# Joining the kv products of two batches, calling the second batch's load three slots sooner, and spacing batch 2's x pieces one and a half units apart

## The chip, the cores and the metric

The kernel runs on one core of one Trainium2 chip. The time is the device time of that core in microseconds (us). Each kernel is run several times; medians and ranges are given. The traced span is 1.7 to 1.9 us shorter than the device time of the same run, so spans are compared only with spans.

## The reference

Linear attention with an RMS norm over each head, then a bilinear feed-forward layer:

```python
# q, k, v: (batch 8, heads 8, seq 576, dim 64); 8*576 = 4608 tokens of 512 features
kv  = np.einsum('bhsd,bhse->bhde', k, v)
out = np.einsum('bhsd,bhde->bhse', q, kv)
x   = out / np.sqrt(np.mean(out*out, axis=-1, keepdims=True) + 1e-06) * g_norm
x   = x.transpose(0, 2, 1, 3).reshape(4608, 512)
y   = (x @ w_a) * (x @ w_b) @ w_out       # w_a, w_b: 512 x 1536, w_out: 1536 x 512
```

## The kernel before

The feed-forward layer goes over the 4608 tokens in 9 strips of 512. A strip is 12 "units" (four products with `wa` and four with `wb`, 1.73 us together) and 4 output groups of 12 products. While strip s runs, attention for batch s+1 is woven into the stream of TensorE in "slots" n, one per unit or group, with half slots in the middle. For batches 2 to 7 the woven pieces are:

- `kv`: one run of 40 small products (128x64 weights, two heads side by side in the two column halves) into PSUM bank 7, then copies to SBUF;
- five x pieces `c` of 128 tokens (the last has 64): `tx` (product and square), `tss` (row sums), `trs` (reciprocal root, and a scaling product on POOL), `txt` (multiply on VectorE, which frees the PSUM bank, and a transposing DMA into `xt`). Piece c uses bank 5 + c % 3, so piece 3 needs the bank of piece 0.

```python
    def load_late(b):                       # on POOL: q, k, v of batch b
        if b > EARLY:
            nc.gpsimd.tensor_copy(gate, qT[(b - 1) % 2][0:1, 0, 0:1])   # waits: q of b-1 transposed
        d = qs_d[b].rearrange("t (h d) -> t h d", h=H)
        for hs in (slice(0, NP), slice(NP, H)):
            nc.gpsimd.dma_start(out=d[:, hs, :], in_=q[b, hs].rearrange("h t d -> t h d"))
        n = 128 * LC
        for t, src in ((ktl[b % 2], k), (vtl[b % 2], v)):
            nc.gpsimd.dma_start(out=t[:, :, 0:LC, :], in_=...)          # 512 rows
            nc.gpsimd.dma_start(out=t[0 : S - n, :, LC, :], in_=...)    # the other 64
    ...
    def slot(A, s, n):
        kb = P[:, 7, 0 : NP * D].rearrange("q (p e) -> q p e", e=D)
        k0, xs = (5, (6.5, 7.5, 8.5, 9.5, 10.5)) if s == 1 else (2, (3.5, 5, 6, 7.5, 8.5))
        if n == k0:
            for p in range(NP):
                A.kv(p, kb[:, p, :])
            A.kv_out(slice(0, NP), kb)
        for c, x in enumerate(xs):
            i = 5 + c % 3
            if n == x:         A.tx(c, i)
            elif n == x + 0.5: A.tss(c)
            elif n == x + 1:   A.trs(c)
            elif n == x + 2.5: A.txt(c, i)
    ...
            if s == 1 and n == 3:
                load_late(3)
            if b + 1 < B and n == (12 if s == 1 else 8):     # b = s + 1
                transpose_q(b + 1)
            if b + 2 < B and n == 13:
                load_late(b + 2)
```

Of the kernel before, what the change touches and what calls it, by code (L numbers as in the profile page):

```python
# [15 lines left out]
def kernel(  # L16
# [11 lines left out]
    nc = tc.nc  # L28

    B, H, S, D = q.shape  # L30
# [5 lines left out]
    NP = H // 2  # L36
# [12 lines left out]
    def sb(shape, dt, name):  # L49
        return pool.tile(shape, dt, name=name, tag=name)  # L50
# [19 lines left out]
    kvb = [sb([128, NP, 128], BF16, f"kvb{i}") for i in range(2)]  # L70
# [34 lines left out]
    P = psum.tile([128, 8, STRIP], FP32, name="P", tag="P")  # L105
# [27 lines left out]
    def load_late(b):  # L133
        if b > EARLY:

            nc.gpsimd.tensor_copy(gate, qT[(b - 1) % 2][0:1, 0, 0:1])
# [5 lines that stand above are left out]
            nc.gpsimd.dma_start(  # L142
                out=t[:, :, 0:LC, :],
                in_=src[b, :, 0:n].rearrange("h (t c) d -> t h c d", c=LC),
            )
            nc.gpsimd.dma_start(
                out=t[0 : S - n, :, LC, :], in_=src[b, :, n:].rearrange("h t d -> t h d")
            )

    def transpose_q(b):  # L150
        nc.sync.dma_start_transpose(qT[b % 2], qs_d[b])


    class Attn:
# [18 lines left out]
                        stop=(c == len(rows) - 1),  # L173
                    )

        def kv_out(self, ps, src):
            for j in range(2):
                r = slice(j * D, (j + 1) * D)
                nc.scalar.copy(kvb[self.b % 2][r, ps, r], src[r])  # L179


        def kv1(self, p, i):
# [118 lines left out]
    class Unit:  # L301
        n = 0
# [36 lines left out]
    def ab_bank():  # L339
        n_ab[0] += 1  # L340
        return AB[(n_ab[0] - 1) % len(AB)]

    def ffn_ab(s, fc, between=None):
        u = Unit(s, fc, ab_bank(), ab_bank())
        u.part_a()
        if between:
            between()
        u.part_b()
# [38 lines left out]
    def ffn_o(s, g, i=O, between=None):  # L387
        o_mm(s, g, i, range(FC // 2))
        if between:
            between()  # L390
        o_mm(s, g, i, range(FC // 2, FC))
        o_out(s, g, i)
# [46 lines left out]
    A = Attn(0)  # L439
# [22 lines left out]
    for j in range(2):  # L462
        r = slice(j * D, (j + 1) * D)
# [7 lines left out]
    for p in range(1, NP):  # L471
        i = X[p % 2]
# [42 lines left out]
    A = Attn(1)  # L515
# [30 lines left out]

    def slot(A, s, n):

        kb = P[:, 7, 0 : NP * D].rearrange("q (p e) -> q p e", e=D)
        k0, xs = (5, (6.5, 7.5, 8.5, 9.5, 10.5)) if s == 1 else (2, (3.5, 5, 6, 7.5, 8.5))  # L550
        if n == k0:
            for p in range(NP):
                A.kv(p, kb[:, p, :])
            A.kv_out(slice(0, NP), kb)
        for c, x in enumerate(xs):
            i = 5 + c % 3
            if n == x:
                A.tx(c, i)
            elif n == x + 0.5:
                A.tss(c)  # L560
            elif n == x + 1:
                A.trs(c)
            elif n == x + 2.5:
                A.txt(c, i)

    for s in range(1, N_STRIP - 1):
        b = s + 1
        A = Attn(b) if b < B else None
        for n in range(FC + 4):
            amid = (lambda n=n: slot(A, s, n - 0.5)) if A else None  # L570
            if n >= FC:
                ffn_o(s, n - FC, ab_bank() if n % 2 else O, amid)
            elif s > 1 or n > 1:
                ffn_ab(s, n, amid)
            if A:
                slot(A, s, n)

            if s == 1 and n == 3:
                load_late(3)
            if b + 1 < B and n == (12 if s == 1 else 8):  # L580
                transpose_q(b + 1)
            if b + 2 < B and n == 13:
                load_late(b + 2)
    last = N_STRIP - 1
    for fc in range(FC):
# [41 lines left out]
```

## Time and profile before

| reading | value | where |
|---|---|---|
| median time | 319.09 us (318.94 to 319.32, 6 runs) | runs |
| TensorE (PE) busy | 310.9 of 317.4 us | page, part 1 |
| a strip with one batch of attention (strip 3, 118.53 to 151.81) | 33.28 us | PE timeline |
| a strip without (strip 7, 251.65 to 282.73) | 31.08 us | PE timeline |
| one kv run of 40 products | 0.85 us | PE timeline |
| PE waits inside strips | two, 1.2 us, both in strip 1 | waits |

Part 1 of the page of the kernel before: busy us, share of the span, and instructions of each engine.

```profile
PE 310.9 (98%) x1907; PEld 147.6 (46%) x1907; DVE 138.2 (44%) x230; ACT 115.8 (37%) x229; POOL 101.8 (32%) x124
```

TensorE bounds it: nothing else is above 46%. So the question is where PE waits. The waits of PE in the kernel before: total us, times, longest us.

```profile
PE P L397 <- DVE eps_t L412: 1.2, 1, 1.2
PE P L258 <- DVE qv L292: 1.2, 2, 0.6
PE P L219 <- ACT sq L215: 0.4, 1, 0.4
```

Only the middle line lies in the strips: the x products (L258) wait for VectorE's `txt` (L292). The timeline of strip 1 of the kernel before shows how; columns are start, us, engine, line, operation, count, and in brackets the idle time before with what ended it.

```profile
68.10 0.72 POOL L146 DMA_DIRECT2D vtl<-in_v_dram  x1
...
68.80 2.08 POOL L282 TENSOR_TENSOR sqt<-rst,g_all 128x512 f32<-128x512 f32 x2
...
69.67 0.69 DVE L330 TENSOR_TENSOR ab<-P,asb 128x512 bf16<-128x512 f32 x1 [0.67 <-PE P L312]
...
70.28 0.68 DVE L292 TENSOR_TENSOR qv<-P,sqt 128x512 bf16<-128x512 f32 x1
...
71.01 0.38 PE L258 MATMUL P<-kvb,qT 128*128 128x128 bf16 x4 [0.58 <-DVE qv L292]
...
72.36 0.69 DVE L330 TENSOR_TENSOR ab<-P,asb 128x512 bf16<-128x512 f32 x1 [0.81 <-ACT sqt L265]
72.97 0.68 DVE L292 TENSOR_TENSOR qv<-P,sqt 128x512 bf16<-128x512 f32 x1
...
73.70 0.38 PE L258 MATMUL P<-kvb,qT 128*64 128x128 bf16 x4 [0.58 <-DVE qv L292]
```

The multiply of piece 0 ends at 70.96, and piece 3, due in the same bank at about 70.27, starts at 71.01. Piece 4 waits for piece 1's multiply in the same way.

POOL issues load 3 until 68.8 and so comes late to the scaling. The two scalings end at 69.9 and 70.9.

One kv run in the stream of PE, strip 3 of the kernel before:

```profile
122.85 1.03 PE L312 MATMUL P<-xt,wb_t 128*128 128x512 bf16 x4
123.81 0.82 PE L168 MATMUL P<-vtl,ktl 128*64 128x64 bf16 x40
124.56 1.04 PE L312 MATMUL P<-xt,wa_t 128*128 128x512 bf16 x4
```

Read starts, not durations (durations are of pipelined instructions). Four 512-wide products take 0.86 us, so without the kv run the next unit would start at 123.71. It starts at 124.56: the run costs 0.85 us, of which 0.10 us passes before its first product.

Now the load of batch 5, on POOL, in the kernel before:

```profile
106.76 1.04 POOL L282 TENSOR_TENSOR sqt<-rst,g_all 64x512 f32<-64x512 f32 x1 [1.19 <-ACT rst L275]
108.85 0.18 POOL L136 COPY gate<-qT 1x1 bf16<-1x1 bf16 x1 [1.05 <-DMA qT<-qs]
109.09 3.31 POOL L139 DMA_DIRECT2D qs<-in_q_dram  x2
112.39 0.91 POOL L142 DMA_DIRECT2D ktl<-in_k_dram  x1
113.29 0.70 POOL L146 DMA_DIRECT2D ktl<-in_k_dram  x1
113.96 0.91 POOL L142 DMA_DIRECT2D vtl<-in_v_dram  x1
```

And the view of the v tile in the same stretch:

```profile
DMA to landing us min/median/max: 12.5/12.7/12.9
```

So v of batch 5 lands at about 126.9 to 127.3 (113.96 + 12.9; its small rest is issued at 114.84). In the kernel before that is early: kv of batch 5 comes in strip 4, at 157.

### The profile page before, as it was taken

The numbers are of one execution on the slowest core, as the hardware profiler recorded it, in microseconds if no ns is written. First come the engines' busy times: TensorE is split into PE (matmuls) and PEld (weight loads), VectorE is DVE, ScalarE is ACT, GpSimd is POOL, SyncE is SP. The second block draws the span as 40 slices with busy tenths as digits, with TensorE's granted clock in tenths as the row PEclk, the third lists the DMA queues.
The fourth block names the chain that finished last, engine by engine and source line by source line (L and its number), as shares of the span: only waits on it lengthen the run. The fifth ranks groups of instructions, "written<-read, shape, count | busy, mean of one in ns | idle before, by whom it ended". The sixth has DMA issues, their size and how long they took to land.

```text
span 317.4 us, 4979 instructions
## 1 busy us (share of the span) xinstructions
PE 310.9 (98%) x1907; PEld 147.6 (46%) x1907; DVE 138.2 (44%) x230; ACT 115.8 (37%) x229; POOL 101.8 (32%) x124
## 2 busy tenths in 40 slices
PE   8999999999999999999999999999999999999995
PEld 3444454444445444544454445444544444444443
DVE  5543345367137613771258225741485144213421
ACT  3733155453246314640355025512461233123310
POOL 8944890193163550347023801310042000000000
PEclk9999999999999999999999999999999999999999
DMA  8999999999799799069916992363012300020002
GB/s 179 196 196 199 200 182 150 228 125 159 167 166 140 128 155 208 4 130 136 228 13 123 124 221 38 69 115 99 2 34 57 116 4 0 33 93 8 0 33 101
DMA packets 94237, 36.19 MB, mean 114 GB/s; under 512 B 64902, under 2 KB 89734, under 8 KB 94214
## 3 DMA queue, kind: packets, MB, share of 16 engines
q0 software_dynamic: 59120, 18.44, 53.4%
q1 hardware_dynamic: 34738, 17.01, 22.9%
q10 hardware_dynamic: 356, 0.43, 0.5%
q8 instruction: 15, 0.25, 0.3%
q14 instruction: 8, 0.07, 0.1%
HBM read 37.78 MB, written 12.98 MB: 160 GB/s over the span
## 4 chain that ended last, share of the span: by engine, by line
PE 85%; DMA 7%; POOL 4%; issue 1%; DVE 1%; ACT 0%; POOLq 0%; DVEq 0%
PE P L312 52%; PE P L369 28%; DMA wb_t<-in_moe_w_b_dram 6%; PE P L258 2%; PE P L168 2%; DMA vt<-in_v_dram 2%; POOL qt L116 1%; POOL wo_t L131 1%; POOL kt L116 1%; POOL vt L116 1%; POOL wa_t L427 0%; POOL wb_t L427 0%; DVE qv L292 0%; PE P L192 0%; PE P L219 0%
## 5 line engine op out<-in xcount | busy, mean ns | idle before, releaser
L330 DVE TENSOR_TENSOR ab<-P,asb 128x512 bf16<-128x512 f32 x108 | 74.5, 691 | 111.3 <-PE P L312 93.8
L312 PE MATMUL P<-xt,wa_t 128*128 128x512 bf16 x432 | 111.9, 379 | 0.0
L312 PE MATMUL P<-xt,wb_t 128*128 128x512 bf16 x432 | 111.7, 379 | 0.1
L326 ACT CAST asb<-P 128x512 bf16<-128x512 f32 x108 | 63.1, 586 | 91.2 <-PE P L312 91.2
L369 PE MATMUL P<-wo_t,ab 128*128 128x512 bf16 (+1 forms) x444 | 95.6, 373 | 0.0
L369 PEld LDWEIGHTS <-ab 128*128 128x128 bf16 x444 | 43.1, 98 | 49.1
L312 PEld LDWEIGHTS <-wa_t 128*128 128x128 bf16 x432 | 41.3, 98 | 47.1 <-issue 0.2
L312 PEld LDWEIGHTS <-wb_t 128*128 128x128 bf16 x432 | 41.2, 98 | 47.2 <-DMA wb_t<-in_moe_w_b_dram 0.6
L282 POOL TENSOR_TENSOR sqt<-rst,g_all 128x512 f32<-128x512 f32 (+1 forms) x24 | 25.0, 1044 | 97.4 <-ACT rst L275 97.4
L382 ACT COPY osb<-P 128x512 f32<-128x512 f32 x17 | 10.0, 586 | 74.2 <-PE P L369 59.6
L384 DVE COPY osb<-P 128x512 f32<-128x512 f32 x18 | 12.4, 691 | 47.2 <-PE P L369 42.6
L139 POOL DMA_DIRECT2D qs<-in_q_dram x12 | 19.8, 1655 | 1.2 <-issue 0.9
L271 DVE TENSOR_REDUCE sst<-sqt 128x8 f32<-128x512 f32 (+1 forms) x24 | 16.2, 676 | 0.8 <-ACT sqt L265 0.8
L292 DVE TENSOR_TENSOR qv<-P,sqt 128x512 bf16<-128x512 f32 (+1 forms) x24 | 16.2, 678 | 0.0
L265 ACT ACTIVATE sqt<-P 128x512 f32<-128x512 f32 (+1 forms) x24 | 14.2, 593 | 1.6 <-PE P L258 1.6
L258 PEld LDWEIGHTS <-qT 128*128 128x128 bf16 (+1 forms) x120 | 8.9, 100 | 9.5 <-issue 4.0
L258 PE MATMUL P<-kvb,qT 128*128 128x128 bf16 (+1 forms) x120 | 11.7, 220 | 1.2 <-DVE qv L292 1.2
L275 ACT ACTIVATE rst<-sst,eps_t 128x8 f32<-128x8 f32 (+1 forms) x30 | 9.0, 301 | 4.3 <-DVE sst L271 4.3
L179 ACT CAST kvb<-P 64x256 bf16<-64x256 f32 (+1 forms) x20 | 6.0, 301 | 11.3 <-PE P L168 11.2
L233 DVE SCALAR_TENSOR_TENSOR xt<-P,g_col,rs 128x288 bf16<-128x288 f32 x16 | 7.5, 512 | 5.2 <-ACT rs L223 5.2
L131 POOL DMA_DIRECT2D wo_t<-in_moe_w_out_dram x12 | 6.4, 533 | 6.7 <-DMA wb_t<-in_moe_w_b_dram 3.2
L282 POOL TENSOR_TENSOR k_x<-rst,g_all 128x512 f32<-128x512 f32 x6 | 6.3, 1044 | 7.0 <-ACT rst L275 7.0
(66 smaller groups left out, 120.4 us busy)
## 6 DMA issues: line engine op xcount, KB each, us to landing
out_dram<-osb SPq DMA_DIRECT2D x23, 256.0 KB, 2.4
qs<-in_q_dram POOLq DMA_DIRECT2D x12, 288.0 KB, 6.9
ktl<-in_k_dram POOLq DMA_DIRECT2D x6, 512.0 KB, 10.1
vtl<-in_v_dram POOLq DMA_DIRECT2D x6, 512.0 KB, 12.5
out_dram<-osb SPq DMA_DIRECT2D x13, 128.0 KB, 2.3
wo_t<-in_moe_w_out_dram POOLq DMA_DIRECT2D x12, 128.0 KB, 5.9
wa_t<-in_moe_w_a_dram POOLq DMA_DIRECT2D x5, 256.0 KB, 9.3
wb_t<-in_moe_w_b_dram POOLq DMA_DIRECT2D x5, 256.0 KB, 9.9
```

Source lines behind the costliest of these rows:

```text
L139: nc.gpsimd.dma_start(out=d[:, hs, :], in_=q[b, hs].rearrange("h t d -> t h d"))
L258: nc.tensor.matmul(P[0:n, i, p * 128 : (p + 1) * 128], lhsT=self.qT[:, p, t0 : t0 + n], rhs=kvb[self.b % 2][:, p, :], start=True, stop=True,)
L265: nc.scalar.activation(sqt[c % 3][0:n], P[0:n, i, :].rearrange("t (h d) -> t h d", h=H), AF.Square)
L271: nc.vector.reduce_sum(sst[c % 3][0:n], sqt[c % 3][0:n], axis=mybir.AxisListType.X)
L282: nc.gpsimd.tensor_mul(sqt[c % 3][0:n], rst[c % 3][0:n].unsqueeze(2).to_broadcast([n, H, D]), g_all[0:n].unsqueeze(1).to_broadcast([n, H, D]),
L292: nc.vector.tensor_mul(t[0:n], P[0:n, i, :].rearrange("t (h d) -> t h d", h=H), sqt[c % 3][0:n])
L312: nc.tensor.matmul(self.a if w is wa_t else self.b, lhsT=w[:, kc, self.fc * 128 : (self.fc + 1) * 128], rhs=xt[:, kc, t0 : t0 + STRIP], st ...
L326: nc.scalar.copy(self.t, self.a)
L330: nc.vector.tensor_mul(abt[self.s % 2][self.fc], self.b, self.t)
L369: nc.tensor.matmul(P[:, i, e0:e1], lhsT=abt[s % 2][fc][:, g * 128 : (g + 1) * 128], rhs=wo_t[:, fc, e0:e1], start=(fc == 0), stop=(fc == F ...
L382: nc.scalar.copy(t, P[:, i, :])
L384: nc.vector.tensor_copy(t, P[:, i, :])
```

## The change

The intent: (1) give piece 3 of batch 2 a bank that is free when it comes, by spacing the pieces; (2) run kv of batches 4 and 5 together in strip 3, and of 6 and 7 in strip 5, in two halves of one bank, so that two entries into and exits from the small products are saved; (3) issue the loads of 5 and 7 earlier, as kv of 5 and 7 is now due a strip earlier, and transpose q of batch 4 earlier so that the gate of load 5 opens in time. (Loads 4 and 6 go from slot 13 to 14; load 4 stays behind the last scaling.)

```diff
-        def kv_out(self, ps, src):
+        def kv_out(self, ps, src, copy=nc.scalar.copy):
...
-        kb = P[:, 7, 0 : NP * D].rearrange("q (p e) -> q p e", e=D)
-        k0, xs = (5, (6.5, 7.5, 8.5, 9.5, 10.5)) if s == 1 else (2, (3.5, 5, 6, 7.5, 8.5))
-        if n == k0:
-            for p in range(NP):
-                A.kv(p, kb[:, p, :])
-            A.kv_out(slice(0, NP), kb)
+        kb = P[:, 7, :].rearrange("q (b p e) -> q b p e", b=2, e=D)
+        k0, xs = (5, (6.5, 8, 9.5, 11, 12.5)) if s == 1 else (2, (3.5, 5, 6, 7.5, 8.5))
+
+        if n == k0 and s in (1, 2, 3, 5):
+            two = [A] if s < 3 else [A, Attn(s + 2)]
+            for i, a in enumerate(two):
+                for p in range(NP):
+                    a.kv(p, kb[:, i, p, :])
+            for i, a in enumerate(two):
+                a.kv_out(slice(0, NP), kb[:, i], nc.vector.tensor_copy if i else nc.scalar.copy)
...
-            if b + 1 < B and n == (12 if s == 1 else 8):
+            if b + 1 < B and n == (12, 4, 8)[min(s, 3) - 1]:
                 transpose_q(b + 1)
-            if b + 2 < B and n == 13:
+            if b + 2 < B and n == (10 if b % 2 else 14):
                 load_late(b + 2)
```

## The prediction

> **What bounds the kernel now.** TensorE. The page shows PE busy 310.9 of 317.4 us (98%), clock 0.999, DVE 44%, ACT 36%. The PE timeline is nearly gapless: a strip with attention takes 33.28 us (118.53 to 151.81), the strip without it 31.08 us (251.65 to 282.73).
>
> **What the change removes.**
> 1. The waits list has one PE wait left in the strips: L258 (the x products) on DVE qv, 2 times, 1.2 us, both in strip 1. The timeline shows why: the loads issued by POOL hold it until 68.8, so the scaling of x piece 0 comes late, its PSUM bank frees at 70.96, and piece 3, due at about 70.27, starts at 71.01. From the kv run to the output products strip 1 takes about 1.34 us more than strip 2 does for the same products (six units, one kv run, five pieces). Pieces one and a half units apart put piece 3 at about 73 us, after its bank is free: -1.34 us.
> 2. Two kv runs fewer. One run of 40 products costs 0.85 us: products start about 16 ns apart (0.65 us), and about 0.2 us goes at the two edges. The Trainium skill, "TensorEngine Tiling (Array Packing)", Key Properties, says that changing the tiling mode drains the engine; this trace agrees with about 0.1 us at each edge. Two merges: -0.4 us.
>
> **What it adds.** kv of batches 5 and 7 is now due a strip earlier. The instruction order on POOL is the same before and after: moving the load from slot 13 to slot 10 passes no POOL instruction. A load starts when the last scaling of the strip is done and the gate (q transposed for the batch before) opens.
> - Batch 5: the gate opened at 108.85; with the earlier transpose the scaling ends it at about 107.8 (old clock). The load's last piece (v) was issued 6 us after the gate and took 12.5 us to land (the v tile's view): needed about 18.5 us after the gate. kv of 5 is due at 123.8+0.65, i.e. 16.6 us after it.
> - Batch 7: the transpose stays at slot 8, gate at 174.87 (old clock), landing at about 193.0; kv of 7 due at 190.36+0.65=191.0.
> So I expect a PE wait on the v load of about 1.9 us twice: +3.8 us. DMA gives no slack: its busy share is 9 tenths while load 5 runs, with 1 MB of output stores among it; the skill, "Trainium Kernel Development and Optimization", Key Constraints, says that all queues share the same 16 engines; two loads with few stores beside them landed sooner (v in about 10 us).
>
> All of these lie on the critical path (PE). Sum: 319.0 - 1.34 - 0.4 + 3.8 = 321.0 us.
>
> **Prediction: 320.8 us, 8 in 10 between 318.2 and 322.0.** Faster by over 2%: 0.01; within 2%: 0.97; slower by over 2%: 0.02.
>
> **What would show it.** Right: no PE wait on DVE qv; new PE idle before the kv line in strips 3 and 5, ended by the DMA of v (or k), 1 to 2.5 us each; strips 4 and 6 about 0.85 us shorter than 33.28. Wrong: kv runs of 80 with no gap before their second half (then about 317.2 us), or a remaining L258 wait in strip 1.
>
> **What would make it wrong.** Loads landing faster (other traffic meets them), q of batch 4 transposed so late amid its own k and v loads that gate 5 opens even later (slower), or the copies of kv holding back something else.

## More of the kernel before

One profiled run of each kernel was traced.

## The result, and the profile after

The changed kernel takes 320.22 us (median of 6 runs, 319.51 to 321.02) against 319.09 us. The ratio is 1.0035, 95% interval 1.0017 to 1.0052: within 2%, and slower. The changed kernel also scatters more: 1.5 us from best to worst, against 0.4 us.

Part 1 of the page of the changed kernel: PE's busy time hardly moved while the span grew from 317.4 to 318.9 us. The time went into waiting, not into work.

```profile
PE 310.2 (97%) x1907; PEld 147.3 (46%) x1907; DVE 140.1 (44%) x234; ACT 114.3 (36%) x225; POOL 101.7 (32%) x124
```

The waits of PE in the changed kernel, its first two lines:

```profile
PE P L168 <- DMA vtl<-in_v_dram: 2.5, 3, 1.1
PE P L397 <- DVE eps_t L412: 1.2, 1, 1.2
```

The wait of x on VectorE is gone; a wait of kv (L168) on the DMA of v is new. In strip 1 of the changed kernel piece 3 comes at 72.73 and the bank was freed by the multiply of piece 0 long before. (The scaling of piece 0 now ends at 68.7, but the multiply again starts 0.61 us after an L330, at 69.94.)

```profile
69.94 0.68 DVE L292 TENSOR_TENSOR qv<-P,sqt 128x512 bf16<-128x512 f32 x1
...
72.73 0.39 PE L258 MATMUL P<-kvb,qT 128*128 128x128 bf16 x4
```

The joined runs in the PE timeline of the changed kernel, in strip 3 and in strip 5:

```profile
122.32 0.82 PE L168 MATMUL P<-vtl,ktl 128*64 128x64 bf16 x40
124.25 1.14 PE L168 MATMUL P<-vtl,ktl 128*64 128x64 bf16 x40 [1.11 <-DMA vtl<-in_v_dram]
125.33 1.04 PE L312 MATMUL P<-xt,wa_t 128*128 128x512 bf16 x4
...
190.27 0.82 PE L168 MATMUL P<-vtl,ktl 128*64 128x64 bf16 x40
192.20 0.32 PE L168 MATMUL P<-vtl,ktl 128*64 128x64 bf16 x8 [1.11 <-DMA vtl<-in_v_dram]
192.83 0.69 PE L168 MATMUL P<-vtl,ktl 128*64 128x64 bf16 x32 [0.32 <-DMA vtl<-in_v_dram]
193.46 1.04 PE L312 MATMUL P<-xt,wa_t 128*128 128x512 bf16 x4
```

In strip 5 the first eight products of batch 7 need the large part of v and the next ones its small rest, and each waits for its own DMA. From the first kv product to the next unit it takes 3.01 us in strip 3 and 3.19 in strip 5. The same run without a wait takes 1.38 us (first experiment below), so 1.63 + 1.81 = 3.44 us are lost. The waits list says only 2.5: it counts idle time after the modelled end of the product before, and misses the part of a wait that is hidden in a stretched run, as in strip 3, where the small rest of v lands at 124.62 (112.12 + 12.5), inside the second half.

Load 5 on POOL in the changed kernel:

```profile
105.28 1.04 POOL L282 TENSOR_TENSOR sqt<-rst,g_all 64x512 f32<-64x512 f32 x1 [1.20 <-ACT rst L275]
106.26 0.18 POOL L136 COPY gate<-qT 1x1 bf16<-1x1 bf16 x1
106.38 3.31 POOL L139 DMA_DIRECT2D qs<-in_q_dram  x2
109.67 0.91 POOL L142 DMA_DIRECT2D ktl<-in_k_dram  x1
110.57 0.70 POOL L146 DMA_DIRECT2D ktl<-in_k_dram  x1
111.25 0.91 POOL L142 DMA_DIRECT2D vtl<-in_v_dram  x1
```

The gate no longer waits; now the last scaling of the strip (ends at 106.3) sets the start. But writing `load_late` at slot 10 and not at 13 did nothing by itself: POOL had no other instruction between. The load starts 2.7 us sooner, of which 1.5 us is the whole stream being ahead after strip 1. The view of the v tile in this stretch:

```profile
DMA to landing us min/median/max: 12.5/12.8/13.0
```

111.25 + 13.0 = 124.25, exactly where the second half of the run starts.

The strips, from start to start in the two PE timelines (us):

| strip | before | after | what differs |
|---|---|---|---|
| 1, from its kv run on | 24.19 | 22.83 | spacing: -1.36 |
| 2 | 33.28 | 33.27 | nothing |
| 3 | 33.28 | 35.53 | +40 products, wait on v |
| 4 | 33.28 | 32.43 | no kv run |
| 5 | 33.28 | 35.71 | +40 products, wait on v |
| 6 | 33.28 | 32.42 | no kv run |

### The profile page after: what moved, and what is told of

It is laid out like the page before. It is cut to its first block, busy times and chain, and to the rows that moved or that the text cites. A ratio compares the mean times of both kernels' runs of the same rounds, so it can differ in the third digit from the quotient of the medians. Undisturbed runs are those within 1.5% of the kernel's fastest.

```text
span 318.9 us, 4981 instructions
## 1 busy us (share of the span) xinstructions
PE 310.2 (97%) x1907; PEld 147.3 (46%) x1907; DVE 140.1 (44%) x234; ACT 114.3 (36%) x225; POOL 101.7 (32%) x124
## 4 chain that ended last, share of the span: by engine, by line
PE 80%; DMA 11%; POOL 6%; issue 1%; ACT 0%; POOLq 0%; ACTq 0%
PE P L312 53%; PE P L369 23%; DMA vtl<-in_v_dram 8%; PE P L258 2%; DMA wb_t<-in_moe_w_b_dram 2%; DMA qT<-qs 1%; PE P L168 1%; POOL qs L139 1%; POOL qt L116 1%; POOL vt L116 1%; POOL kt L116 1%; POOL ktl L142 1%; POOL vtl L142 1%; PE P L192 0%; POOL wa_t L427 0%
## 5 line engine op out<-in xcount | busy, mean ns | idle before, releaser
L330 DVE TENSOR_TENSOR ab<-P,asb 128x512 bf16<-128x512 f32 x108 | 74.5, 691 | 104.3 <-PE P L312 86.1
L384 DVE COPY osb<-P 128x512 f32<-128x512 f32 x18 | 12.5, 692 | 46.5 <-PE P L369 41.9
L179 ACT CAST kvb<-P 64x64 bf16<-64x64 f32 (+1 forms) x16 | 4.6, 285 | 13.8 <-PE P L168 13.7
## 6 DMA issues: line engine op xcount, KB each, us to landing
vtl<-in_v_dram POOLq DMA_DIRECT2D x6, 512.0 KB, 12.4
```

The source lines that it names most:

```text
L330: nc.vector.tensor_mul(abt[self.s % 2][self.fc], self.b, self.t)
L384: nc.vector.tensor_copy(t, P[:, i, :])
```

## The experiments

The theory: the spacing and the joining each save what they were meant to, and kv of 5 and 7 comes due before v has landed, because the load starts late (behind the strip's last scaling and the gate), issues q first, and shares the DMA engines with the output stores. The main rival: the joined run itself costs the time, with two batches in one bank and two engines copying from it. All kernels below gave correct results.

### k and v ahead of q

Same bytes, same start, another order of the issues (batch 2 keeps the old order).

```diff
-        for hs in (slice(0, NP), slice(NP, H)):
-            nc.gpsimd.dma_start(out=d[:, hs, :], in_=q[b, hs]...)
         for t, src in ((ktl[b % 2], k), (vtl[b % 2], v)):
             ...
+        for hs in (slice(0, NP), slice(NP, H)):
+            nc.gpsimd.dma_start(out=d[:, hs, :], in_=q[b, hs]...)
```

> The changed kernel, but for batches 3 to 7 k and v are loaded ahead of q; same bytes, same start of the load. Late-load theory: v lands some 4 us sooner, before kv is due, no PE wait on v, joined runs cost 1.4 us each: 320.2 - 3.4 = about 317.0 us (316.8 to 317.5). Rival (the joined run of 80 products itself costs this, its two halves sharing one bank with two copies): 320 us as before, gap in the run kept. A third outcome, q now late for its transpose, would show as PE waiting on qT.

Measured: 317.26 us (317.08 to 317.51, 5 runs), ratio to the kernel before 0.9947 (0.9934 to 0.996). v of batch 5 is issued at 108.27 and lands 12.4 us later, at 120.7. The PE timeline of this kernel, strip 3 (the edit shifts line numbers by 7):

```profile
122.33 1.46 PE L175 MATMUL P<-vtl,ktl 128*64 128x64 bf16 x80
123.71 0.82 PE L319 MATMUL P<-xt,wa_t 128*128 128x512 bf16 x3
```

All 80 products in one go, 1.38 us, with the same bank, the same copies and the same joining. The rival falls. The scatter is back to 0.4 us. No wait on `qT` appeared: q lands later, but is transposed late enough.

### The joined run one unit later

The loads untouched; kv and the x pieces of strips 3 and 5 moved by one unit.

```diff
-        k0, xs = (5, (...)) if s == 1 else (2, (3.5, 5, 6, 7.5, 8.5))
+        k0, xs = (5, (...)) if s == 1 else (3, (4.5, 6, 7, 8.5, 9.5)) if s in (3, 5) else (2, (3.5, 5, 6, 7.5, 8.5))
```

> The changed kernel with the joined kv runs and the x pieces of strips 3 and 5 one unit (1.73 us) later; loads untouched. Late-load theory: v lands at the same time after its gate, kv is due 1.73 us later, so the lost 1.6 and 1.8 us fall to about 0.0 to 0.2 us each: about 317.1 us. Rival (the joined run itself): about 320 us.

Measured: 317.34 us (317.19 to 317.77, 5 runs), ratio 0.9949 (0.9937 to 0.9961). No PE product waits on v; v still takes 12.8 and 12.3 us to land. The other side of the same race was moved, with the same outcome.

### The two parts alone

Spacing alone, on the kernel before:

```diff
-... (5, (6.5, 7.5, 8.5, 9.5, 10.5)) if s == 1 ...
+... (5, (6.5, 8, 9.5, 11, 12.5)) if s == 1 ...
-            if b + 2 < B and n == 13:
+            if b + 2 < B and n == (14 if s == 1 else 13):
```

> The kernel before with only batch 2's x pieces one and a half units apart (and load 4 kept behind the last scaling). Spacing theory: the wait of x on a late bank goes, -1.36 us as in the strip times of the two traces: 317.7 us, no PE wait on DVE qv. Rival (the spacing only moves the wait to ACT or DVE further on, and the gain in the changed kernel came from elsewhere): about 319 us.

Measured: 317.55 us (317.5 to 317.88, 5 runs), ratio 0.9957 (0.9945 to 0.9969), and no PE wait on VectorE.

Joining and loads alone: the changed kernel with `(6.5, 7.5, 8.5, 9.5, 10.5)` put back.

> The changed kernel with the old spacing of batch 2's pieces; joined kv runs and moved loads stay. If the parts add: 320.2 + 1.36 = 321.6 us, that is +2.5 us on the kernel before, with PE waiting on the v load twice (about 1.6 and 1.8 us of lost time). Rival (the two parts depend on each other, the earlier strip 2 being what outruns the loads): nearer 320 us, with smaller waits on v.

Measured: 321.79 us median of 6 runs, ratio 1.0097 (1.0072 to 1.0122). The median hides two kinds of run: four with a mean granted clock of 0.999 or 1.0 took 321.02, 321.02, 321.76 and 321.83 us (mean 321.4, where 321.6 was expected), and two with a clock of 0.993 and 0.994 took 323.31 and 323.70. The traced run is one of the latter. Its stretches in strip 5 (us from the span's start: length, busy time of PE, PEld, DVE, ACT, POOL, then granted clock, DMA share, GB/s):

```profile
192.00:193.00 1.00, 0.00 (x0) 0.00 (x0) 0.00 (x0) 0.00 (x0) 0.00 (x0) 1.00 1.06 101
193.00:194.00 1.00, 0.41 (x13) 0.30 (x14) 0.00 (x0) 0.00 (x0) 0.00 (x0) 0.94 0.10 7
194.00:195.00 1.00, 1.00 (x33) 0.94 (x33) 0.00 (x0) 0.00 (x0) 0.00 (x0) 0.50 0.00 0
195.00:196.00 1.00, 1.00 (x3) 0.33 (x4) 0.22 (x1) 0.73 (x2) 0.00 (x0) 0.50 0.00 0
196.00:197.00 1.00, 1.00 (x3) 0.30 (x2) 0.63 (x2) 0.17 (x1) 0.00 (x0) 0.50 0.00 0
197.00:198.00 1.00, 1.00 (x5) 0.45 (x4) 0.00 (x0) 0.41 (x1) 0.00 (x0) 0.85 0.00 0
```

After a wait of 1.61 us on v the granted clock fell to 0.50. Finer stretches put the fall at 193.9, 0.4 us after PE had resumed, and the return at 197.3: 3.4 us at half speed, so some 1.7 us were lost beyond the wait. The first wait was smaller than expected in this trace (strip 3 takes 34.89 us, 0.98 more than without a wait). In the medians and the mean above, the parts add when the clock holds: -1.4 for the spacing and +2.4 for the rest, against +1.1 for both. The second cost, by the clock, is new.

### The gate of load 5 as late as before

```diff
-            if b + 1 < B and n == (12, 4, 8)[min(s, 3) - 1]:
+            if b + 1 < B and n == (12, 8, 8)[min(s, 3) - 1]:
```

> The changed kernel with q of batch 4 transposed in slot 8 of strip 2 again (as before the change) instead of slot 4. Late-load theory: the gate of load 5 opens about 1 us later, as in the kernel before, and the time lost before kv of batch 5 grows from 1.6 to about 2.6 us; kv of batch 7 is as it was: 321.2 us. Rival (that move was of no use): 320.2 us.

Measured: 322.10 us median of 6 runs, ratio 1.0094 (1.0068 to 1.012). Again two kinds: 320.80, 321.61 and 321.63 us at a clock of 0.999 or 1.0 (mean 321.35; 321.2 was expected), and 322.56, 323.41 and 323.52 us at 0.993 to 0.995. In the trace (a run of the first kind) the gate is open at 107.58 and not at 106.26, 1.3 us later, and the wait before kv of batch 5 is 2.23 + 0.27 us where it was 1.11. A delay of the load's start shows up nearly one for one in PE's wait. The earlier transpose in the change was of use; it was too small.

### The output stores out of the load's way, first try

```diff
-        store(s * STRIP + g * 128, t, 0, d_model)
+        if s in (2, 4):
+            held.append((s * STRIP + g * 128, t))
+        else:
+            store(s * STRIP + g * 128, t, 0, d_model)
...
+            if n == 5:                       # in the next strip
+                while held:
+                    store(*held.pop(0), 0, d_model)
```

> The changed kernel, loads and kv runs untouched, but the output stores of strips 2 and 4 are issued in the next strip, after its kv run, so that 1 MB less shares the DMA engines with loads 5 and 7. If sharing is what makes v take 12.3 to 13 us from its issue: about 10 us, as in the loads with few stores beside them; v then lands before kv is due, no wait on v, about 317.1 us. If the stores do not matter and only the late start does: landing stays above 12 us, wait stays, 320.2 us.

Measured: 320.24 us, ratio 1.0032 (1.0018 to 1.0045), v landing after 13.1 us: like the changed kernel. But this tells nothing. The timeline of the sync engine's queue in this kernel shows the stores where they always were:

```profile
110.34 7.99 SPq L362 DMA_DIRECT2D out_dram<-osb  x5
```

Between the old place and slot 5 of the next strip this engine has no other instruction, so moving the call moved nothing. It is the same mistake as expecting something from moving `load_late` from slot 13 to slot 10.

### The output stores out of the load's way, second try

The same with `n == 7`, which puts the stores behind the next strip's first x transpose on that engine.

> Second try of the deferred stores (in the first, the stores stayed next in the sync engine's own order, and so left at the same time as before). Now the stores of strips 2 and 4 stand behind the first x transpose of the next strip, which the order of instructions shows; they cannot leave before about 134 and 202 us. If sharing the DMA engines with the stores is what makes v take 12.3 to 13 us: v lands in about 10 us, before kv is due, no wait on v, about 317.1 us. If sharing does not matter: landing above 12 us and 320.2 us.

Measured: 317.15 us (317.06 to 317.38, 5 runs), ratio 0.9941 (0.9928 to 0.9955). The queue of the sync engine, and then the DMA issues in the stretch of load 5 (KB each, us to landing), both of this kernel:

```profile
134.00 2.68 SPq L362 DMA_DIRECT2D out_dram<-osb  x5
```

```profile
ktl<-in_k_dram POOLq DMA_DIRECT2D x1, 512.0 KB, 7.8
vtl<-in_v_dram POOLq DMA_DIRECT2D x1, 512.0 KB, 9.3
```

With POOL issuing v at the same time (111.36) as in the changed kernel (111.25), v lands in 9.3 us and not in 13.0; for batch 7 in 8.8 and not 12.3. No wait is left. One MB of stores among the load cost it about 3.6 us. (In this trace some product records are missing, so its PE counts are a little low.)

### Two runs or one

On the k-and-v-ahead version, kv of the second batch in a run of its own, one unit later.

```diff
+        if n == k0 + 1 and s in (3, 5):
+            a = Attn(s + 2)
+            for p in range(NP):
+                a.kv(p, kb[:, 1, p, :])
+            a.kv_out(slice(0, NP), kb[:, 1], nc.vector.tensor_copy)
```

> The k-and-v-ahead-of-q version (317.26 us) with the two batches' products in two runs one unit apart instead of one run, everything else the same. If joining saves the two edges of a run, some 0.2 us twice: strips 3 and 5 are 0.2 us longer each, 317.65 us. If joining saves nothing: 317.26 us and equal strips.

Measured: 317.59 us (317.52 to 317.91, 5 runs) against 317.26 with one run. From output group to output group, strips 3 and 5 take 34.14 us each where the joined version takes 33.91 and 33.92. Joining saves 0.23 + 0.22 = 0.45 us, in the traces; the two kernels ran in different jobs, so their medians (0.33 us apart) are the weaker evidence.

### The last x piece at full width

The last piece of a batch has 64 tokens and so 128*64 weights. Here it is computed 128 tokens wide, overlapping the piece before, and only its upper 64 rows are used. On the k-and-v-ahead version.

```diff
+            r = slice(128 - n, 128)                    # n = 64 for the last piece
             for p in range(NP):
                 nc.tensor.matmul(
-                    P[0:n, i, p * 128 : (p + 1) * 128],
-                    lhsT=self.qT[:, p, t0 : t0 + n],
+                    P[:, i, p * 128 : (p + 1) * 128],
+                    lhsT=self.qT[:, p, t0 + n - 128 : t0 + n],
...                                                      # and [r] for [0:n] in all that follows
```

> The k-and-v-ahead-of-q version with the last x piece of each batch computed 128 tokens wide, overlapping the piece before, and only its upper 64 rows used; results the same, no 128*64 tiling in it. If the edges come from changing the tiling mode: its four products take 0.22 us of the stream and not 0.44, six times: 317.26 - 1.3 = 315.95 us. If they come from something else (the products, the bank): 317.3 us.

Measured: 315.91 us (315.88 to 315.94, 4 runs), ratio to the kernel before 0.9895 (0.9879 to 0.9911). This is the fastest version. Six pieces gave 1.35 us (317.26 - 315.91), 0.22 us each, by doing twice the arithmetic. What it removed is the stretch of narrow (128*64) products. That the 0.22 us is a drain at the change of tiling mode is only argued; the run shows the cost, not the drain.

## Why the prediction was right

- **What bounds the kernel, and the sign.** PE stayed at 97 to 98% with nearly the same busy time; 320.8 us was forecast and 320.22 measured, inside 318.2 to 322.0. The signs it named came: no PE wait on `qv`, a wait on v before the second half of both joined runs, and strips 4 and 6 0.85 us shorter.
- **Spacing: -1.34 us forecast.** The traces give -1.36; alone it gives 1.44 us in the medians (318.99 for the kernel before in the same job, 317.55 with the spacing). The size and the remedy were right, the reason was not, and that is luck: the prediction has POOL's late scaling hold the bank, and in the trace VectorE's own order holds it (above). The spacing cures that too, as piece 3 now comes two slots after the multiply and not half a slot. No run moved load 3 alone; the traces decide this.
- **Joining: -0.4 us forecast.** 0.45 in the traces. It is real, and the smallest of the terms. The Trainium skill ("TensorEngine Tiling (Array Packing)", Key Properties) says that a change of tiling mode drains the engine. The runs agree with it: a stretch of other tiling costs 0.22 us besides its products, for four products (full-width experiment) as for 40 (two runs or one).
- **Wait on v: +3.8 us forecast.** 3.44 us in the traced run. This is the term that was most out: v was expected 1.9 us late twice, and cost 1.63 and 1.81. The prediction reckoned with the last part of v, its small rest. For batch 5 that landed 12.5 us after its issue as forecast, at 124.62, and was due at about 122.97, so it was 1.65 us late and not 1.85; the issue came 5.86 us after the gate and not 6.0, and kv was due 16.7 us after it and not 16.6. For batch 7 it landed at 192.81, 1.9 us late. The traced run (320.62 us) is one of the slower of the six: in the medians (320.22 against 317.26 with k and v ahead) the wait costs only about 3 us. The sum, -0.12 (an earlier start of strip 1, by chance: that start lies between 60.80 and 61.09 in all the traces) - 1.36 - 0.45 + 3.44 = +1.5 us, is the difference of the two spans, 318.9 - 317.4.
- **"Moving the load from slot 13 to slot 10 passes no POOL instruction."** Right. The change set out to bring the loads forward and brought only load 5 forward, by the earlier transpose; load 7 not at all (its gate still opens 0.5 us after the last scaling).
- **"DMA gives no slack."** The Trainium skill ("Trainium Kernel Development and Optimization", Key Constraints; also "DMA: Bandwidth & Descriptors", Issuing engines are not separate DMA queues) says that DMAs of all queues share 16 engines and interleave. The deferred stores show it: 13.0 us became 9.3.
- **What the prediction lacked.** That the granted clock can fall after such a wait. None of the six runs of the changed kernel shows it (0.998 to 1.0). The two versions with the old spacing and with the late gate have a lower mean clock (0.993 to 0.995) in five of their twelve runs, and one of these five was traced. The length of the wait alone does not decide it: the traced run with the late gate waited 2.23 us and kept a clock of 1.00. What makes the clock fall was not isolated.

Shown by runs: that the wait on v is the whole loss (four edits that touch only k and v's order, the due time, or the stores remove it or, for the gate, lengthen it). Only argued: that the scatter of the changed kernel, 1.5 us, is the scatter of v's landing; it is 0.1 to 0.6 us in the versions without the wait, but single runs were not traced, and the kernel before, which has no such wait, once took 320.31 us among eleven runs.

## What to carry to other kernels

When work is pulled forward, its inputs must be pulled forward too, and a DMA moves only if its issue passes another instruction on its own engine or is released sooner: look at the engine's order and at the gate, not at the line of the source. The same holds for a late result: before another engine is blamed, look at what stood before the instruction on its own engine. Of the bytes that are loaded together, issue first what is due first, and ask what other traffic shares the engines just then. In a stream of products that is already gapless, look for changes of tiling mode: it can pay to compute more than is needed in the same mode (1.35 us here).

## What the Trainium skill lacked or had wrong

- "TensorE: Matmul & The Clock Gate", Back-to-back issue gap, gives about 131 ns a product for a sustained stream at N=512 and 81 ns at N=128. Here 48 products of 512 take 10.36 us, 216 ns each, at clock 1.00, and four of 128 take 0.22 us, 55 ns each: its figures for isolated products fit the stream, those for the stream do not.
- The same page ("Wait — 56ns, not 53.3ns?") says that starts are never closer than about 25 ns, however small N is. Forty more kv products of N=64, alternating between two column halves, lengthen a run from 0.75 to 1.38 us: 16 ns each. The statement needs an exception for products in different parts of the array, which the page's own Part 3 describes as running at the same time.
- The same page, Part 1, has the clock fall after an idle window of about 3.4 us. Here it fell to 0.50 after a wait of 1.61 us on v (the wait lies between short runs of small products; whether those counted as activity was not tested), in some runs of a kernel only, and it stayed at 1.00 after a wait of 2.23 us in the traced run with the late gate.
- "TensorEngine Tiling (Array Packing)" says that a mode change drains the engine but gives no cost: the two-runs and the full-width experiments show 0.22 us for each stretch of another tiling.
- "DMA: Bandwidth & Descriptors" says that all queues share the engines but not what that costs one load: v landed 13.0 us after its issue beside 1 MB of stores, and 9.3 us without.
